# Transfer sizes at the two ends of a streaming group norm: halves and a whole where there were quarters

## The chip, the cores and the metric

The kernel runs on one core of a Trainium2 chip (trn2). The metric is device time in microseconds (us) of one execution; lower is better. Times of one table row were taken on the same chip in alternating rounds unless I say otherwise.

## The reference

```python
# x: (128, 1024, 32, 16) bf16, g, b: (1024,) bf16; 32 groups of 32 channels
xr  = x.reshape(B, G, C // G, H, W)
mu  = xr.mean(axis=(2, 3, 4), keepdims=True)
var = ((xr - mu) ** 2).mean(axis=(2, 3, 4), keepdims=True)
xn  = ((xr - mu) / jnp.sqrt(var + 1e-5)).reshape(B, C, H, W)
return xn * g[None, :, None, None] + b[None, :, None, None]
```

134 MB are read once and 134 MB written once. A group is 32 channels of 512 elements, and it lies whole in one partition.

## The kernel before

There are 32 tiles, each of 128 partitions (4 images x 32 groups) by 16384 bf16 elements: 4 MB, 32 KB per partition. The tile is normalised in place, in one of six buffers. TensorE sums a tile by 32 matmuls with the identity, ScalarE (ACT) makes the sum of squares, and the 32 scalings (one for each channel) are shared by VectorE (DVE, 22), GpSimd (POOL, 8) and ACT (2). All large transfers are issued from one queue, SyncE's (SP), in program order. Most tiles are loaded and stored whole. At the ends they go in quarters of the columns, so that the first sum and the last store may start early:

```python
    def L(i):                                        # load of tile i
        xt = xpool.tile([P, F], BF16, name="xt")     # F = 16384
        parts = NQ if i == 0 or i >= NT - 1 else 1   # NQ = 4, NT = 32
        w = F // parts
        for c in range(parts):
            chain("sp", nc.sync.dma_start(
                out=xt[:, c*w:(c+1)*w], in_=x_v[i][:, c*w:(c+1)*w]))
    ...
    def in_parts(i):
        return i >= NT - STORE_IN_PARTS              # the last two tiles

    def A(i):                                        # scaling, and the last two stores
        if not in_parts(i):
            ...                                      # 8 on POOL, 22 on DVE
            return
        for c in range(NQ):
            for k in range(c * KQ, (c + 1) * KQ):
                on_act = i == NT - 1 and k >= (c + 1) * KQ - ACT_SHARE
                scale_on("act" if on_act else "dve", i, k)
            S(i, c, c + 1)                           # store of quarter c
            if c == NQ // 2 - 1 and i + 1 < NT:
                R1(i + 1)                            # full sum of the next tile

    def finish(i):                                   # inner tiles
        ...                                          # 2 scalings on ACT
        S(i, 0, NQ)                                  # store, whole
        j = i + AHEAD                                # AHEAD = 5
        if UPFRONT <= j < NT:
            L(j)                                     # waits until its buffer is stored
```

(Cuts are marked by `...`; calls are folded to fewer lines.)

## Time and profile before

| | before |
|---|---|
| median time | 635.31 us (five runs, 635.03 to 635.89) |
| span of the profiled run | 633.4 us |
| DMA busy | 39 of 40 slices at 9 tenths |
| ACT, DVE, PE, POOL busy | 82, 58, 46, 36% |
| first / last DMA engine done with the last store | 623.75 / 632.41 us |

The page of the profile has, in this order: the DMA engines' mean busy tenths and their rate in 40 equal slices; packets; packets, megabytes and share by queue; the chain that ended last, by engine and then by line; DMA issues with their count, size, and time from issue to landing.

```profile
DMA  9999999999999999999999999999999999999995
GB/s 367 433 431 419 430 431 430 430 433 430 430 434 433 435 431 429 431 430 428 431 435 426 433 439 439 431 426 433 430 435 430 430 435 430 433 423 439 431 418 228
DMA packets 11062, 268.69 MB, mean 424 GB/s; under 512 B 1312, under 2 KB 1312, under 8 KB 1312
...
q1 hardware_dynamic: 10944, 268.44, 98.8%
q8 instruction: 8, 0.13, 0.1%
q14 instruction: 14, 0.11, 0.0%
...
DMA 71%; ACT 10%; PE 9%; DVE 3%; issue 3%; POOL 1%; SPq 0%; DVEq 0%; ACTq 0%; POOLq 0%
...
xt<-in_x_dram SPq DMA_DIRECT2D x30, 4096.0 KB, 29.2
out_dram<-xt SPq DMA_DIRECT2D x30, 4096.0 KB, 38.3
xt<-in_x_dram SPq DMA_DIRECT2D x8, 1024.0 KB, 16.4
out_dram<-xt SPq DMA_DIRECT2D x8, 1024.0 KB, 18.8
```

The DMA engines are the limit, at 430 GB/s or so from beginning to end; no compute engine is full. Only the last slice is half empty. The windows view (start and end, width, busy time and instructions of PE (TensorE), PEld (its weight loads), DVE, ACT and POOL, share of full speed that TensorE's clock was granted, DMA share, GB/s) resolves it:

```profile
622.00:624.00 2.00, 0.00 (x0) 0.00 (x0) 0.00 (x0) 0.00 (x0) 0.00 (x0) 0.50 0.96 406
624.00:626.00 2.00, 0.00 (x0) 0.00 (x0) 0.00 (x0) 0.00 (x0) 0.00 (x0) 0.50 0.62 262
626.00:628.00 2.00, 0.00 (x0) 0.00 (x0) 0.00 (x0) 0.00 (x0) 0.00 (x0) 0.50 0.26 111
628.00:630.00 2.00, 0.00 (x0) 0.00 (x0) 0.00 (x0) 0.00 (x0) 0.00 (x0) 0.50 0.13 53
630.00:632.00 2.00, 0.00 (x0) 0.00 (x0) 0.00 (x0) 0.00 (x0) 0.00 (x0) 0.50 0.06 25
```

A share of 0.06 is one engine of 16. So the engines don't end together: one of them works alone for the last microseconds. Two more kinds of record in the trace are used below. A packet record has start, duration and size. A semaphore update is written by each engine when it is done with its share of a transfer, so a large transfer has 16 landings. I call the distance from the first to the last of the 16 the *lag*.

### The profile page before, as it was taken

What the parts mean: (1) busy time and instruction counts of PE and PEld (TensorE: products, weight loads), DVE (VectorE), ACT (ScalarE), POOL (GpSimd) and SP (SyncE); (2) the same over time, 40 slices, a digit from 0 to 9 for tenths busy, and PEclk for the clock granted to TensorE, in tenths of its full rate; (3) what the DMA queues carried; (4) which work ended last, traced back from release to release, by engine and by line L of the source; (5) the groups of instructions that cost most, each with busy time, mean ns of one, the idle gap of its engine ahead of it and who ended that gap; (6) DMA issues with size and microseconds to landing.
All of it is one profiled execution on the core that took longest, in us unless ns stands there. A gap on an engine that the chain in (4) does not pass through costs nothing.

```text
span 633.4 us, 3906 instructions
## 1 busy us (share of the span) xinstructions
PE 289.4 (46%) x1025; PEld 113.3 (18%) x1025; DVE 368.9 (58%) x825; ACT 518.1 (82%) x238; POOL 228.4 (36%) x373
## 2 busy tenths in 40 slices
PE   5577604663345633456423655235553355547000
PEld 2223201221112211122101222012221122212000
DVE  0077777767744577545675455754557645567760
ACT  4599999999977798777987788977879778797960
POOL 0044444444442244422444333443324433244100
PEclk9789758766787667876668776687866678668655
DMA  9999999999999999999999999999999999999995
GB/s 367 433 431 419 430 431 430 430 433 430 430 434 433 435 431 429 431 430 428 431 435 426 433 439 439 431 426 433 430 435 430 430 435 430 433 423 439 431 418 228
DMA packets 11062, 268.69 MB, mean 424 GB/s; under 512 B 1312, under 2 KB 1312, under 8 KB 1312
## 3 DMA queue, kind: packets, MB, share of 16 engines
q1 hardware_dynamic: 10944, 268.44, 98.8%
q8 instruction: 8, 0.13, 0.1%
q14 instruction: 14, 0.11, 0.0%
q10 hardware_dynamic: 96, 0.00, 0.0%
HBM read 134.22 MB, written 134.22 MB: 424 GB/s over the span
## 4 chain that ended last, share of the span: by engine, by line
DMA 71%; ACT 10%; PE 9%; DVE 3%; issue 3%; POOL 1%; SPq 0%; DVEq 0%; ACTq 0%; POOLq 0%
DMA out_dram<-xt 41%; DMA xt<-in_x_dram 30%; PE pa L166 9%; ACT ja L244 9%; DVE xt L368 3%; ACT xt L363 1%; SPq L101 0%; POOL scl L337 0%; PE pb L166 0%; POOL shift L343 0%; ACT rstd L308 0%; DVE jd L189 0%; DVE rstd L312 0%; POOL bia L353 0%; DVE jv L292 0%
## 5 line engine op out<-in xcount | busy, mean ns | idle before, releaser
L244 ACT ACTIVATE ja<-xt,negmean 128x8192 fp8e5<-128x8192 bf16 x60 | 426.7, 7112 | 74.7 <-DVE jd L189 74.7
L166 PE MATMUL pa<-xt,eye 128*128 128x512 bf16 x976 | 278.6, 456 | 294.6 <-DMA xt<-in_x_dram 294.6
L368 DVE TENSOR_SCALAR xt<-xt,scl,bia 128x512 bf16<-128x512 bf16 x716 | 341.3, 552 | 39.8 <-POOL bia L353 39.8
L166 PEld LDWEIGHTS <-eye 128*128 128x128 bf16 x1024 | 113.2, 113 | 470.8 <-DMA xt<-in_x_dram 295.9
L368 POOL TENSOR_SCALAR xt<-xt,scl,bia 128x512 bf16<-128x512 bf16 x240 | 190.5, 805 | 3.3
L337 POOL TENSOR_SCALAR scl<-gb,rstd 128x32 f32<-128x32 f32 x31 | 11.1, 358 | 337.0 <-DVE rstd L312 337.0
L189 DVE TENSOR_SCALAR_CACHE_REDUCE jd<-pa 128x512 bf16<-128x512 f32 x32 | 22.0, 688 | 172.3 <-PE pa L166 172.3
L363 ACT ACTIVATE xt<-xt,bia,scl 128x512 bf16<-128x512 bf16 x68 | 50.8, 798 | 0.8 <-DVE bia L324 0.8
L244 ACT ACTIVATE ja<-xt,q 128x4096 fp8e5<-128x4096 bf16 x8 | 29.7, 3708 | 7.0 <-DVE jd L189 6.8
L312 DVE RECIPROCAL rstd<-rstd 128x1 f32<-128x1 f32 x32 | 5.1, 160 | 24.6 <-ACT rstd L308 24.6
L343 POOL TENSOR_SCALAR shift<-scl,negmean 128x32 f32<-128x32 f32 x31 | 11.1, 358 | 3.1
L166 PE MATMUL pb<-xt,eye 128*128 128x512 bf16 x48 | 11.0, 379 | 1.0 <-DMA xt<-in_x_dram 1.0
L244 ACT ACTIVATION_READ_ACCUMULATOR ja<-xt,negmean 128x1 f32 x60 | 11.2, 186 | 0.0
L308 ACT ACTIVATE rstd<-s,v 128x1 f32<-128x1 f32 x30 | 8.8, 295 | 2.8
L353 POOL TENSOR_TENSOR bia<-shift,gb 128x32 f32<-128x32 f32 x31 | 7.8, 251 | 2.6
L216 POOL TENSOR_SCALAR off<-negmean,q 128x1 f32<-128x1 f32 x2 | 0.9, 430 | 20.6 <-DVE jd L189 20.6
L308 ACT ACTIVATE rstd<-var,eps_t 128x1 f32<-128x1 f32 x2 | 0.6, 294 | 7.5 <-DVE jv L292 7.5
L273 POOL TENSOR_SCALAR v<-s 128x1 f32<-128x1 f32 x30 | 5.7, 191 | 2.5
L156 DVE COPY gb<-gb_p 128x64 f32<-128x64 f32 x1 | 0.2, 225 | 5.3 <-PE gb_p L148 5.3
L116 ACT ACT_TABLE_LOAD x1 | 1.3, 1283 | 1.7 <-PEq L444 1.7
L189 DVE DVE_READ_ACCUMULATOR jd<-pa 128x1 f32 x32 | 2.6, 81 | 0.0
L292 DVE TENSOR_SCALAR_CACHE_REDUCE jv<-sq,seed 128x4 f32<-128x4 f32 x2 | 0.4, 216 | 2.9 <-ACT ja L244 2.9
(18 smaller groups left out, 6.1 us busy)
## 6 DMA issues: line engine op xcount, KB each, us to landing
xt<-in_x_dram SPq DMA_DIRECT2D x30, 4096.0 KB, 29.2
out_dram<-xt SPq DMA_DIRECT2D x30, 4096.0 KB, 38.3
xt<-in_x_dram SPq DMA_DIRECT2D x8, 1024.0 KB, 16.4
out_dram<-xt SPq DMA_DIRECT2D x8, 1024.0 KB, 18.8
gb_b<-in_g_dram ACTq DMA_DIRECT2D x1, 2.0 KB, 3.4
gb_b<-in_b_dram ACTq DMA_DIRECT2D x1, 2.0 KB, 5.4
```

Source lines behind the costliest of these rows:

```text
L116: chain("act", nc.scalar.activation(out=warm[:], in_=eps_t[:], func=ACT.Sqrt))
L166: nc.tensor.matmul(out=ps[:], lhsT=eye[:], rhs=st["xt"][:, k * MMN : (k + 1) * MMN], start=(k == lo), stop=(k == hi - 1),),
L189: nc.vector.tensor_scalar(out=jd[:], in0=ps[:], scalar1=-inv_n, scalar2=seed, op0=ALU.mult, op1=ALU.add, accum_out=total[:],),
L244: nc.scalar.activation(out=ja[:, 0:w], in_=st["xt"][:, k * w : (k + 1) * w], func=ACT.Square, bias=bias, scale=scale, accum_out=sq, satura ...
L273: nc.gpsimd.tensor_scalar(out=v0[:], in0=s0[:], scalar1=inv_n, scalar2=EPS, op0=ALU.mult, op1=ALU.add,),
L308: nc.scalar.activation(out=rstd[:], in_=last_sum[:], func=ACT.Sqrt, bias=bias[:], scale=scale),
L312: chain("dve", nc.vector.reciprocal(out=rstd[:], in_=rstd[:]))
L337: nc.gpsimd.tensor_scalar(out=scl[:], in0=gam, scalar1=rstd[:], scalar2=None, op0=ALU.mult),
L343: nc.gpsimd.tensor_scalar(out=shift[:], in0=scl[:], scalar1=st["negmean"][:], scalar2=None, op0=ALU.mult,),
L353: nc.gpsimd.tensor_tensor(out=bia[:], in0=shift[:], in1=bet, op=ALU.add),
L363: inst = nc.scalar.activation(out=span, in_=span, func=ACT.Identity, bias=bia, scale=scl)
L368: inst = eng.tensor_scalar(out=span, in0=span, scalar1=scl, scalar2=bia, op0=ALU.mult, op1=ALU.add,)
```

## The change

Its intent is fewer and larger transfers at the ends, as large transfers are cheaper by the byte: load 0 and the stores of tiles 30 and 31 in halves (2 MB), load 31 whole (4 MB).

```diff
-        parts = NQ if i == 0 or i >= NT - 1 else 1
+        parts = 2 if i == 0 else 1
@@
+        HQ = NQ // 2
         for c in range(NQ):
             for k in range(c * KQ, (c + 1) * KQ):
                 on_act = i == NT - 1 and k >= (c + 1) * KQ - ACT_SHARE
                 scale_on("act" if on_act else "dve", i, k)
-            S(i, c, c + 1)
+            if c % HQ == HQ - 1:
+                S(i, c + 1 - HQ, c + 1)
```

The order of the instructions on PE, ACT, DVE and POOL is unchanged.

## The prediction

> **What bounds the kernel now.** The DMA engines. The page's slices show all 16 busy in 39 of 40 slices (mean 424 GB/s); ACT, the busiest compute engine, is busy 82%. The chain of waits is 71% DMA. In the trace's packet records a packet is one partition row, and each starts where the one before it on that engine ends: 32 KB takes 1213 ns, 8 KB 309 ns (medians). Per engine, 60 whole transfers x 8 rows x 1.213 = 582.2 us, 16 quarters x 8 x 0.309 = 39.6 us, and 76 completion writes x 9 ns = 0.7 us: 622.5 us, after a first packet at 1.8 us. The first engine to finish the last store does so at 623.75 us: it is never out of work. The last finishes at 632.4, 8.65 us behind, having lost about 1 us at each of some eight steps through the run, close to the eight 16 KB instruction fetches (947 to 1069 ns) in the packet records. The span ends at 633.4.
>
> **What the change does.** Same bytes; the order of PE, ACT, DVE and POOL is unchanged. Sync issues 67 large transfers instead of 76.
> - Load 31: 32 rows of 8 KB per engine become 8 of 32 KB: 9.89 to 9.70 us, -0.18.
> - Load 0, stores 30 and 31: 96 rows of 8 KB become 48 of 16 KB. By a straight line through the two measured sizes (301 ns per 8 KB plus 8 ns) I estimate 610 ns each: 29.66 to 29.29 us, -0.37.
> - Nine completion writes fewer: -0.08.
> Sum: -0.63 us on every engine's stream, all critical, as the stream is gapless.
>
> The Trainium skill, "DMA: Bandwidth & Descriptors", section "Anatomy of one DMA", gives about 2 us fixed per DMA. Nine fewer would save 18 us if serial. Here several transfers are queued, and no gap stands between packets.
>
> **What it delays, and why that is hidden.**
> - Start: the first matmul waits for the first half, 8.2 instead of 5.8 us; the first squares end at about 27.8, while the step after them waits for tile 1's sum at 31.5 anyway. Store 0 goes out at 45 us, with loads queued to 57.
> - Last load: whole at about 583 us, when its last quarter lands now. Tile 31's sum is then done at about 592; its partial sum, at 587.5, is in time for the squares at 590.1, the full one for its use at 596.7.
> - Stores: tile 30's first half is issued at about 596.9 (its first quarter at 594 now); the first-finishing engine gets to it at 604.2. Tile 31's halves go out at about 611 and 614.8; that engine reaches them at about 613.8 and 618.7. Margins 7, 3 and 4 us, and 8 more on the slowest engine, which decides. The last store is queued behind work, so the end isn't lengthened.
>
> **Prediction: 634.7 us, 634.0 to 635.4 eight times in ten.** Faster by over 2%: 0.005; within 2%: 0.985; slower: 0.01.
>
> **What would show each step.** 16 KB packets of about 610 ns; the earliest engine's finish of the last store near 623.1 us and the latest near 631.8; the lag still about 8.6 us; DMA busy at 9 tenths up to the last slice; the first DVE scaling still at about 34 us; the last compute instruction still ending near 614.8.
>
> **What would make it wrong.** A 16 KB packet that costs more than twice an 8 KB one; fetches falling otherwise, so that the slowest engine's lag changes by a microsecond; a slower ramp, as each engine's first packet is twice as long; or tile 31's first half issued over 3 us late, so that an engine idles. A run-to-run shift of 0.3 us would hide the gain; the three runs before spread by 0.12 us.

## The result and the profile after

| five runs each | before | after |
|---|---|---|
| median | 635.31 us | 634.70 us |
| range | 635.03 to 635.89 | 634.07 to 634.99 |

Executions over 1.5% slower than the fastest of the same kernel are left out of the means. The ratio is 0.999, with a 95% interval of 0.9977 to 1.0004. (A ratio is the mean time of one kernel's fast runs over that of the other's fast runs of the same rounds, so not quite the ratio of the medians.) That is "the same" at the 2% mark, as predicted, and the median is the predicted 634.7; but the interval still includes 1.

The same lines of the page after the change:

```profile
DMA  8999999999999999999999999999999999999995
GB/s 365 433 432 423 431 429 430 437 427 431 439 430 433 429 431 429 430 433 431 427 439 428 431 435 435 433 432 433 431 431 435 430 433 433 433 431 430 434 424 222
DMA packets 9766, 268.69 MB, mean 424 GB/s; under 512 B 1168, under 2 KB 1168, under 8 KB 1168
...
q1 hardware_dynamic: 9648, 268.44, 98.7%
...
xt<-in_x_dram SPq DMA_DIRECT2D x31, 4096.0 KB, 29.4
out_dram<-xt SPq DMA_DIRECT2D x30, 4096.0 KB, 38.3
out_dram<-xt SPq DMA_DIRECT2D x4, 2048.0 KB, 18.4
xt<-in_x_dram SPq DMA_DIRECT2D x2, 2048.0 KB, 9.8
```

There are 1296 packets fewer, the rate is the same, and the last slice is as empty as before. The first slice reads 8 tenths instead of 9, which the prediction did not foresee; load 0 is taken up below. In the windows of the end, the same staircase:

```profile
622.00:624.00 2.00, 0.00 (x0) 0.00 (x0) 0.00 (x0) 0.00 (x0) 0.00 (x0) 0.50 0.82 352
624.00:626.00 2.00, 0.00 (x0) 0.00 (x0) 0.00 (x0) 0.00 (x0) 0.00 (x0) 0.50 0.42 180
626.00:628.00 2.00, 0.00 (x0) 0.00 (x0) 0.00 (x0) 0.00 (x0) 0.00 (x0) 0.50 0.23 98
628.00:630.00 2.00, 0.00 (x0) 0.00 (x0) 0.00 (x0) 0.00 (x0) 0.00 (x0) 0.50 0.13 57
630.00:632.00 2.00, 0.00 (x0) 0.00 (x0) 0.00 (x0) 0.00 (x0) 0.00 (x0) 0.50 0.04 16
```

What was delayed at the start can be followed in the timeline (start, duration, engine, line, operation, and in brackets the idle time before and what ended it). Before:

```profile
5.78 3.44 PE L166 MATMUL pa<-xt,eye 128*128 128x512 bf16 x8 [5.78 <-DMA xt<-in_x_dram]
...
21.49 3.71 ACT L244 ACTIVATE ja<-xt,q 128x4096 fp8e5<-128x4096 bf16 x1
...
31.53 0.69 DVE L189 TENSOR_SCALAR_CACHE_REDUCE jd<-pa 128x512 bf16<-128x512 f32 x1 [15.40 <-PE pa L166]
...
32.40 0.29 ACT L308 ACTIVATE rstd<-var,eps_t 128x1 f32<-128x1 f32 x1 [7.11 <-DVE jv L292]
```

After:

```profile
8.39 3.57 PE L166 MATMUL pa<-xt,eye 128*128 128x512 bf16 x8 [8.39 <-DMA xt<-in_x_dram]
...
24.23 3.71 ACT L244 ACTIVATE ja<-xt,q 128x4096 fp8e5<-128x4096 bf16 x1
...
31.78 0.69 DVE L189 TENSOR_SCALAR_CACHE_REDUCE jd<-pa 128x512 bf16<-128x512 f32 x1 [13.12 <-PE pa L166]
...
32.65 0.29 ACT L308 ACTIVATE rstd<-var,eps_t 128x1 f32<-128x1 f32 x1 [4.62 <-DVE jv L292]
```

The first matmul starts 2.6 us later, and so do the squares. By the square root this has become 0.25 us: the idle time in front of it (7.11, now 4.62 us) has absorbed the rest. At the end, the halves of tile 31 go out at 610.9 and 614.8 us. The engine that finishes first reaches them at 613.4 and 618.3, so even that engine never ran dry.

Landings in the two profiled runs (us):

| | first engine | last engine | lag |
|---|---|---|---|
| before, end of the last store | 623.75 | 632.41 | 8.65 |
| after, end of the last store | 623.16 | 632.01 | 8.85 |

### The profile page after: what moved, and what is told of

It reads as the page before. It is cut to its first block, busy times and chain, and to the rows that moved or that the text cites. A ratio compares the mean times of both kernels' runs of the same rounds, so it can differ in the third digit from the quotient of the medians.

```text
span 633.0 us, 3886 instructions
## 1 busy us (share of the span) xinstructions
PE 290.0 (46%) x1025; PEld 113.5 (18%) x1025; DVE 369.7 (58%) x825; ACT 518.0 (82%) x238; POOL 229.3 (36%) x373
## 4 chain that ended last, share of the span: by engine, by line
DMA 69%; ACT 14%; PE 8%; DVE 3%; issue 2%; POOL 0%; SPq 0%; DVEq 0%; ACTq 0%; POOLq 0%
DMA out_dram<-xt 42%; DMA xt<-in_x_dram 26%; ACT ja L244 13%; PE pa L166 8%; DVE xt L368 3%; ACT xt L363 1%; POOL scl L337 0%; SPq L101 0%; DVE jd L189 0%; ACT rstd L308 0%; POOL shift L343 0%; DVE rstd L312 0%; DVE jv L292 0%; DVEq L457 0%; DVE bia L324 0%
```

## The experiments

The theory to test, "the stream": each DMA engine works through its list without a gap, so a change is worth the packet overhead it saves and nothing else, and what the parts do for the compute engines is hidden. Rivals: (A) nothing is saved, the 0.6 us are noise; (B) each DMA costs a fixed 2 us or so (a figure whose source is named under e3); (C) the parts at the ends matter because they start the first sum and the last store early.

### e1_after_again: the changed kernel once more

No edit; nine runs of the kernel before beside it.

> The changed kernel once more, to narrow the interval. Stream theory (each DMA engine works without a gap, so the change saves its packet overhead, 0.63 us): 0.6 us under the kernel before, ratio 0.9990, with 0.3 us either way for the lag of the slowest engine. Rival A (nothing is saved, the first look was noise): ratio 1.0000. Rival B (a fixed cost of about 2 us for each of the nine DMAs removed): 18 us under.

Measured: median 635.25 (634.59 to 635.71) against 635.46 (635.04 to 635.65); ratio 0.9997, interval 0.9984 to 1.0009. First engine done at 623.45, last at 632.11. Taking the ten runs of the changed kernel from both sessions together, and the 14 of the kernel before, the means are 634.94 and 635.40: 0.46 us apart, with a standard error of 0.16 us (0.69 in the first session alone, 0.21 in the second). So B is out by far. The stream theory's 0.63 us lies about one standard error from this; a smaller saving fits as well. A is unlikely, not excluded by this run alone.

### e2_whole: no parts at all

```diff
-        parts = 2 if i == 0 else 1
+        parts = 1
-            if c % HQ == HQ - 1:
-                S(i, c + 1 - HQ, c + 1)
+            if c == NQ - 1:
+                S(i, 0, NQ)
```

> Goes on from the changed kernel: first load, last load and the last two stores all whole, no part transfers at all. Stream theory: 61 rather than 67... here 64 transfers of 32 KB rows; per engine another 48 packets of 611 ns become 24 of 1213, -0.2 us, and 3 completion writes less; the last store, issued at about 615 us, comes when the slowest engine has 7 us of work left: 634.4 to 634.7 us, 0.8 us under the kernel before. Rival C (the parts at the two ends matter, since they let the first sum and the last store start early): the last half of tile 31 leaves no earlier but the first half leaves 4 us later, so 2 to 5 us over the changed kernel. Shown by the compute start (first matmul at about 13 us instead of 8) and by whether engines idle near 615 us.

Measured: median 635.51 (634.66 to 635.72), kernel before 635.46; ratio 0.9999, interval 0.9987 to 1.0012. The further gain of 0.2 us isn't there, and it would be too small to see. But rival C asked for 2 to 5 us over the changed kernel, and that isn't there either, although the last store was now issued at 615.3 us. The windows of the end show why:

```profile
618.00:620.00 2.00, 0.00 (x0) 0.00 (x0) 0.00 (x0) 0.00 (x0) 0.00 (x0) 0.50 1.18 508
620.00:622.00 2.00, 0.00 (x0) 0.00 (x0) 0.00 (x0) 0.00 (x0) 0.00 (x0) 0.50 0.72 311
622.00:624.00 2.00, 0.00 (x0) 0.00 (x0) 0.00 (x0) 0.00 (x0) 0.00 (x0) 0.50 1.14 492
624.00:626.00 2.00, 0.00 (x0) 0.00 (x0) 0.00 (x0) 0.00 (x0) 0.00 (x0) 0.50 0.72 311
626.00:628.00 2.00, 0.00 (x0) 0.00 (x0) 0.00 (x0) 0.00 (x0) 0.00 (x0) 0.50 0.27 115
```

(Shares over 1, and the swing between neighbours, are probably an artefact: a 32 KB packet counted whole in one window.) The fast engines did run dry: the first was done with tile 30 at 614.28, before the last store was issued, and ended the last store at 626.26 instead of 623.16. The slowest was done with tile 30 only at 622.84 and took 9.66 us for the last store, its normal pace; it ended at 632.50. The engines that wait are not the one that ends last.

### e3_all_quarters, e6_pieces_one_dma: more DMAs, or smaller packets

The saving of the change is too small to take apart, so these two do the opposite sixtyfold. In e3 every load and store goes in quarters (256 DMAs instead of 76, all rows 8 KB):

```diff
-        parts = NQ if i == 0 or i >= NT - 1 else 1
+        parts = NQ
@@ finish
-        S(i, 0, NQ)
+        for c in range(NQ):
+            S(i, c, c + 1)
```

> The kernel before with every load and store in quarters of the columns: 256 DMAs of 8 KB rows, none of 32 KB. Stream theory: each of the 60 transfers split costs every engine 8 x (4 x 309 - 1213) = 184 ns and 3 completion writes of 9 ns, 0.21 us; times 60 is 12.7 us: 648 us. Rival B (2 us for each of 180 more DMAs): about 995 us. Rival A (packet size is free when queued): 635 to 637 us.

In e6 the 76 DMAs stay, but a gap in the tile cuts each row of each whole transfer in four packets of 8 KB:

```diff
-        xt = xpool.tile([P, F], BF16, name="xt")
+        xt = xpool.tile([P, NQ, QF + PAD], BF16, name="xt")   # PAD = 32
@@ loads; stores and compute likewise
-                    out=xt[:, c * w : (c + 1) * w], in_=x_v[i][:, c * w : (c + 1) * w]
+                    out=xt[:, c * n : (c + 1) * n, 0:QF],
+                    in_=x_v[i][:, c * n * QF : (c + 1) * n * QF].rearrange("p (a f) -> p a f", a=n),
```

> The kernel before with 76 DMAs as it has, but each row of a whole transfer cut in four packets of 8 KB (the tile in the on-chip memory has a gap of 64 bytes after each quarter row, so that pieces can't join). If the size of the packet costs: close to the run with quarters everywhere, 642 to 644 us. If the number of DMAs costs: the time of the kernel before, 635.4 us.

| | median us | before, same rounds | ratio (95%) | pace of the first engine, us for one tile transfer |
|---|---|---|---|---|
| kernel before | | | | 9.684 |
| e6: small packets | 640.30 (four runs) | 635.38 | 1.0080 (1.0066 to 1.0094) | 9.793 |
| e3: small packets, more DMAs | 643.98 (four runs) | 635.46 | 1.0135 (1.0120 to 1.0151) | 9.83 |

The pace is the time between landings on the first engine, over some 45 tile transfers from 110 to 555 us (for e3, four quarters of 2.457). The windows view of that stretch, for the kernel before, e6 and e3, ends with the rate:

```profile
110.00:550.00 440.00, 208.32 (x722) 80.89 (x723) 264.87 (x573) 370.66 (x164) 172.61 (x276) 0.72 1.00 432
```

```profile
110.00:550.00 440.00, 204.89 (x694) 80.02 (x709) 265.03 (x572) 366.84 (x162) 173.47 (x276) 0.71 1.01 427
```

```profile
110.00:550.00 440.00, 207.21 (x716) 79.42 (x715) 261.59 (x569) 364.34 (x160) 172.49 (x271) 0.72 1.01 426
```

Both packets and DMAs cost, and both little. From e6, 24 more packets per engine and transfer cost 0.109 us: 4.5 ns each. From e3 against e6, three more DMAs cost about 0.035 us: 12 ns each. In e3 all 180 more DMAs together with the packets cost 8.5 us, so one more DMA cannot have cost more than 48 ns. The Trainium skill ("DMA: Bandwidth & Descriptors", section "Anatomy of one DMA") gives a fixed 2 us per DMA, and puts most of it down to the wait for completion. The section is about DMAs issued from GpSimd, while all large ones here come from SyncE, so it was only a rival to test. In a queue that always has a next transfer hardly any of it shows here.

I had expected 12.7 us from e3 and got 8.5. The expectation took packet durations for pace: 8 x 1213 + 9 = 9713 ns, where the engine's pace is 9684. Packet records overlap by a few nanoseconds, which inflates a sum over short packets most.

### e4_row_blocks, e7_row_halves: a control that failed, and why

e4 was to be the control for e3: as many DMAs, but rows of 32 KB, by cutting each whole transfer in four blocks of 32 partitions.

```diff
+        if parts == 1:
+            for r in range(0, P, 32):                 # e7: 64
+                chain("sp", nc.sync.dma_start(out=xt[r:r+32, :], in_=x_v[i][r:r+32, :]))
+            ...
@@ finish
-        S(i, 0, NQ)
+        for r in range(0, P, 32):
+            chain("sp", nc.sync.dma_start(out=o_v[i][r:r+32, :], in_=state[i]["xt"][r:r+32, :]))
```

> The kernel before with each of the 60 whole transfers split in four blocks of 32 rows: the same 256 DMAs as with quarters everywhere, but every row still 32 KB. Stream theory, in which the size of the packet costs and the number of DMAs hardly does: 180 x 9 ns = 1.6 us over the kernel before, 637 us. If the number of DMAs costs and not the packets: the same as quarters everywhere, 648 us.

Measured: four runs from 733 to 948 us, three of them slow against the fastest. Neither expectation was near. e7 asked why:

> The kernel before with each whole transfer cut in rows 0 to 63 and 64 to 127, to find why four blocks of 32 rows took 842 us. Port theory (Trainium skill, SBUF page: both halves reach only 8 of 16 memory ports): the rate in the first 100 us is again near 208 GB/s, and the time well over 700 us. Rival (each DMA gives an engine too little work, 64 KB): with 128 KB per engine the excess halves or vanishes, first 100 us well over 208 GB/s.

One run, so of unknown state: 752.12 us. From 16 to 110 us, in the windows view, the kernel before, e4 and e7:

```profile
16.00:110.00 94.00, 50.44 (x192) 20.28 (x191) 58.65 (x131) 86.45 (x40) 38.15 (x62) 0.79 1.00 427
```

```profile
16.00:110.00 94.00, 34.65 (x128) 13.70 (x128) 40.08 (x88) 62.77 (x29) 28.12 (x46) 0.74 1.00 208
...
200.00:500.00 300.00, 119.22 (x418) 46.08 (x417) 149.14 (x325) 205.65 (x89) 99.30 (x156) 0.69 1.00 370
```

```profile
16.00:110.00 94.00, 33.58 (x126) 13.63 (x128) 40.89 (x90) 63.11 (x29) 28.44 (x47) 0.74 1.00 208
...
200.00:500.00 300.00, 136.02 (x463) 53.00 (x471) 161.80 (x350) 224.34 (x98) 105.55 (x168) 0.69 1.00 406
```

The rate is half, 208 GB/s, in both, though e7's DMAs give each engine twice as much work as e4's. That speaks against the rival and agrees with the Trainium skill, "SBUF — State Buffer", section "Door 1: The DMA port swizzle": partitions 0 to 31 and 0 to 63 both reach 8 of the 16 ports of the on-chip memory. Later the rate recovers to 370 and 406 GB/s. The lags had grown by then, from under 1 us in the first 50 us to 15 us and more, so the engines were at different blocks at the same time, and so presumably at both sets of ports; this last step is argued, not shown. As a control for the count of DMAs e4 was spoiled, and e6 took its place.

### e5_half_matmuls: does the fetch of matmul instructions make the slowest engine?

The prediction laid the 8.65 us of lag to the eight 16 KB fetches in the packet records. The Trainium skill ("Runtime: NRT & Kernel Launch", section "Instruction fetch mechanics") says that an engine's instructions come in blocks of 16 KiB, 256 of them, through a DMA queue of their own. Queue q8 agrees: 8 packets, 0.13 MB, one each 78 us or so, which is four tiles of 64 PE instructions. So e5 leaves out every other matmul of the inner tiles (the mean of half the data). Its output is wrong, which doesn't matter for the time.

```diff
-        for k in range(lo, hi):
+        for k in range(lo, hi, step):               # step = 2 for inner tiles, sum doubled
```

> The changed kernel with every other matmul of the 30 inner tiles left out and the sum doubled (the mean is then that of half the data: wrong on purpose). Theory: what sets the end beyond the stream is the lag of the slowest DMA engine, 8.7 us, fed by the 16 KB fetches of the matmul engine's instructions, one each 78 us. Half the instructions give 4 fetches, that engine falls back some 4 us less, and the next engine (7 us behind) then ends last: 1.5 to 2 us under the changed kernel, 633.0 us. Rival: the lag comes from something else, and the time stays within 0.5 us of the changed kernel.

Measured: median 635.90 (635.17 to 636.44), ratio to the kernel before 1.001 (0.9996 to 1.0024). Four fetches on q8, as expected; lag of the slowest engine 8.98 us, and no gain. (The rival's 0.5 us was missed too: this median is 1.2 us over the changed kernel's first and 0.65 over its second, in other sessions; why is open.) The other engines did gain: the 16 lags at the end add up to 34 us, against 45 in the changed kernel (42 in e1). So each of these fetches falls on some engine, but they don't pile up on the slowest one. My theory of the lag fell.

### e8_probe: which engine is the slowest

The last half store gives up its last 256 columns, which go in 16 small stores of 1, 2, ... 15 and 8 rows. The Trainium skill ("DMA: Bandwidth & Descriptors", section "Why a DMA increments its semaphore by 16 and not by 1") says that such a store of n rows runs on the n lowest-numbered engines.

```diff
+            if i == NT - 1 and c == NQ - 1:
+                probe(i)        # (0:128, F/2:F-256), then rows r:r+n of the last 256 columns
```

> The changed kernel, with the last 256 columns of the last store cut in 16 small stores of 1 to 15 and 8 rows. By the Trainium skill a store of n rows, n up to 16, goes to the n lowest-numbered engines; so the landings of these stores tell how far each numbered engine is behind at the end. Expected: the time within 1 us of the changed kernel, and one engine of one number 8 to 9 us behind the first.

Landings of the first four: one row at 623.19; two rows 623.37 and 626.96; three rows 623.55, 625.48, 627.13; four rows 623.72, 625.65, 627.30 and 632.38. The slowest engine, 9.2 us behind, is number 3, if the numbering holds. The time was a miss: 639.44 us (one run), because each later probe waited for the completion of an older transfer before it could be issued.

### e9_dve_doubled: the new theory of the lag

The last landing of a transfer, in the kernel before, falls behind its pace at eight places after 110 us. The five near 231, 319, 407, 505 and 603 us, of 0.78 to 0.96 us each, all follow an 8 KB fetch on queue q14 (at 225, 313, 402, 499, and 593 or 595 us). Those fetches are some 90 us apart. A block of 8 KB is 128 instructions if 16 KiB are 256 (an estimate from the page named in e5); DVE runs 825 instructions for 32 tiles, 26 each, so 128 last about five tiles or 95 us. So: the slowest engine is the one that fetches for DVE. e9 doubles the scalings on DVE (same result):

```diff
+        n = 2 if key == "dve" else 1                 # two instructions of 256 columns
+        for m in range(n):
+            w = HW // n
+            scale_part(key, i, k, k * HW + m * w, k * HW + (m + 1) * w)
```

> The changed kernel with each scaling on the vector engine done as two instructions of 256 columns instead of one of 512 (same result, some 720 more instructions). New theory of the end: the slowest DMA engine is the one that serves the vector engine's instruction fetches of 8 KB, each of which cost it about 0.96 us (the steps of the last landing stand beside them). 720 instructions more are some 5.6 fetches more, so the lag of the slowest engine grows from 8.9 to about 14 us and the time to about 640 us. If the lag has another cause: 635 us, lag under 10 us. Vector time stays under the 19.4 us that a tile takes either way.

Measured: median 639.70 (639.52 to 640.46, four runs), ratio 1.0069 (1.0055 to 1.0083). On the page, the instructions of each engine and the fetches, first in the changed kernel and then in e9:

```profile
PE 290.0 (46%) x1025; PEld 113.5 (18%) x1025; DVE 369.7 (58%) x825; ACT 518.0 (82%) x238; POOL 229.3 (36%) x373
...
q14 instruction: 14, 0.11, 0.0%
```

```profile
PE 291.0 (46%) x1025; PEld 113.8 (18%) x1025; DVE 470.3 (74%) x1541; ACT 518.3 (81%) x238; POOL 235.2 (37%) x373
...
q14 instruction: 20, 0.16, 0.1%
```

Six more fetches; the slowest engine now steps back each 38 to 57 us, still by 0.8 to 1.0 us, and ends at 636.69 us: 4.7 us later than in the changed kernel. Its lag at 565 us is 11.6 us (8.1 in the changed kernel); the expected 14 was not reached, 12.7 at 610 us was the most. At the very end the lag shrinks to 4.6, because the compute of the last tile ends late (626 us) and the fast engines wait for it; the slowest doesn't. A DVE fetch costs that engine 0.8 to 1.0 us: 309 ns for its own packet, and the rest in the data packet after it, which takes longer (1865 instead of 1213 ns after the fetch at 499 us, in the kernel before).

### e10_pool_share, e12_pool_share_again, e11_act_pool_share: a better version

```diff
-POOL_SHARE = 8
+POOL_SHARE = 12
-LAST_SHARE = 2          # e11 only
+LAST_SHARE = 4
```

This leaves DVE 18 scalings per tile (e10 and e12) or 16 (e11), and so fewer instructions to fetch. (POOL gets more, 493 instead of 373, and q14 still has 14 packets in all three.)

> The changed kernel with 12 instead of 8 of each tile's 32 scalings on the gpsimd engine, 18 instead of 22 on the vector engine. By the same theory one fetch less of the vector engine's instructions: lag of the slowest engine about 8, time 0.5 to 1 us under the changed kernel, if the engine that serves gpsimd's fetches doesn't take over as the slowest. If the lag has another cause: no difference.

> The same kernel as e10_pool_share, which had 634.27 us but a spread of 2 us in five runs: is its gain on the kernel before real? Theory: 0.8 to 1.5 us under the kernel before. If the first look was chance: under 0.5 us.

> The changed kernel with 12 of each tile's 32 scalings on gpsimd and 4 on the scalar engine, 16 left on the vector engine (22 before). By the theory that the vector engine's fetches make the slowest DMA engine, two fewer of them: 1 to 1.9 us under the changed kernel, 633.0 to 634.0 us, unless another engine's lag, or the scalar engine's longer chain, takes over. If the lag has another cause: no difference.

| five runs each | median us | range | before, same rounds | ratio (95%) |
|---|---|---|---|---|
| e10 | 634.27 | 633.68 to 635.74 | 635.52 | 0.9979 (0.9965 to 0.9992) |
| e12 | 633.84 | 633.39 to 634.65 | 635.39 | 0.9980 (0.9967 to 0.9994) |
| e11 | 633.57 | 633.38 to 634.52 | 635.39 | 0.9976 (0.9963 to 0.9988) |

All three intervals lie below 1: 0.2% under the kernel before, a little, but real, and more than the change itself gives. The lag at the end is 7.30 us in e12 and 8.06 in e11 (8.85 in the changed kernel). In e10 the profiled run was the slowest of the five, 635.74 us, with a lag of 9.59. So the times agree with the theory, while the traces of single runs scatter too much to prove that fewer DVE fetches are the reason; e9 shows only what more of them cost. e11 brought nothing sure over e12.

The landings show a limit that these versions meet. In e10 the last landing still steps back by 0.9 to 1.0 us after the q14 fetches at 364, 481 and 583 us. In e11 and e12 it makes no step over 0.5 us after 300 us: another engine ends last there, one that falls back by about 0.2 us at every second transfer. It is in the changed kernel too, 7.46 us behind at the end, second to last. In e12 it ends 7.30 us behind and in e11 8.06, while the engine beside DVE's fetches, the last but one, is 6.6 and 7.6 us behind. So in the changed kernel's trace fewer DVE fetches could gain about 1.4 us at most (8.85 - 7.46). What slows the second engine was not asked.

## Why the prediction was right

**The limit.** It named the gapless stream on the slowest DMA engine, and that held: first engine 623.1 predicted, 623.16 measured; slowest 631.8 and 632.01; 16 KB packets 610 and 611 ns.

**What is hidden.** It said that the later start and the later stores cost nothing. The first half had landed by 8.35 us (matmul at 8.39, 8.2 predicted), the squares ended at 27.9 (27.8 predicted), the last load was whole by 582.8 (583), the halves went out at 610.9 and 614.8 (611 and 614.8). e2 strengthens this: even with no parts at all, nothing is lost, because the slowest engine has 7.5 us of work left when the last store is issued (615.3 to 622.84). The parts at the ends buy nothing in either kernel.

**The size of the gain.** The sum of -0.63 us was too large. That the median came out on 634.7 was luck: e1, the same kernel, gave 635.25, and the two sessions together -0.46 us. Three terms, as the prediction put them, and the first engine's landings:

| term | predicted | measured |
|---|---|---|
| load 31 whole | -0.18 us | -0.21 (9.88 before, 9.67 after) |
| stores 30 and 31 in halves | two thirds of -0.37 | -0.11 (19.52 before, 19.41 after); -0.16 in e1 |
| load 0 in halves | one third of -0.37 | +0.11 (landed by 12.56 before, 12.67 after); +0.03 in e1 |

The sum is about -0.2 to -0.3 us. Two steps failed. Packet durations were added as if they were pace; by the paces of e3 and e6, a packet less is worth 4.5 ns and not 8, and a DMA less 12 ns (9 in the prediction), which for 72 packets and 9 DMAs fewer per engine makes 0.43 us. And the first packets of 16 KB took longer to get going, which the prediction had named as a risk: load 0 gains nothing. The measured difference, 0.46 us with a standard error of 0.16, is near that 0.43 us, but isn't explained term by term. Single runs differ by as much where the stores first join the loads: from the landing near 51 us to the next took 10.22 us before, 9.97 after, and 10.31 in e1, the same kernel as the latter.

**The lag.** "Close to the eight 16 KB instruction fetches" was a coincidence of number and size, and e5 refuted it. By the steps beside them, five 8 KB fetches of DVE's instructions make 4.3 of the 8.65 us, and e9 shows that such fetches set that engine back. The rest is not explained: 2.8 us had already built up by 113 us. This didn't hurt the prediction, as the change leaves both kinds alone.

## What to carry to other kernels

When the DMA queue never runs dry, whether the transfers at the ends are quarters, halves or wholes is worth a few tenths of a microsecond; first look at when the slowest engine, not the mean, gets to the piece you want to send early. If one engine of 16 ends alone, look for what only that engine carries: here half of its lag came with the instruction stream of a compute engine that was only 58% busy. The versions that took instructions off that engine (e10 to e12) were 0.2% faster than the kernel before, though it isn't shown that this is why; and the next engine, 1.4 us ahead in the changed kernel, ended last in e11 and e12. And cut transfers by columns, not by partitions: 32 or 64 partitions at a time halved the rate at first.

## What the Trainium skill lacked or had wrong

- "Runtime: NRT & Kernel Launch" calls the cost of crossing a fetch block mostly hidden, and gives 16 KiB as the block. In a kernel bound by DMA it isn't hidden: a fetch for DVE set the engine that serves it back by 0.8 to 1.0 us each time, and five such steps, 4.3 us, were half of the 8.65 us by which the last engine trailed. Only q8's packets were 16 KB; q14's 14 were of 8 KB.
- "DMA: Bandwidth & Descriptors": its 2 us fixed cost is given for a DMA issued from GpSimd, and no figure says what a DMA from SyncE costs behind others in a queue. Here 180 more of them, with four times the packets, cost 8.5 us in all; about 12 ns per DMA and 4.5 ns per packet by the paces.
- The same page names engines 7 and 15 as usually the slower ones, and ties that to DMAs issued from GpSimd. It names none for SyncE's; here it was number 3, if stores of few rows go to the lowest-numbered engines as that page says (e8).
- "SBUF — State Buffer", "Door 1": the halved rate agrees (208 against 427 GB/s). The page doesn't have that transfers queued one behind another recover part of it (370 and 406 GB/s after 200 us).
- No page says that the lag between DMA engines adds up over a run (0.6 us at 4 us, 8.65 at the end), nor that it hides late stores at the end.
